# A convolution and mixture-of-experts kernel: the third sort's scatters leave one by one instead of six in a row

## The chip, the cores and the metric

The kernel runs on one core of one Trainium2 chip. The metric is device time in microseconds (us) of one execution; lower is better. The core has TensorE (PE, matrix products and transposes), VectorE (DVE), ScalarE (ACT), GpSimd (POOL) and SyncE (SP, which issues most transfers).

## The reference, cut to what matters

A long convolution over the sequence, by FFT, and then a mixture of experts that sends each token to one expert:

```python
# _attn_ref: x (8, 5696, 128), h (5696, 128)
y = irfft(rfft(x, 2*S) * rfft(h, 2*S))[:, :S, :]
# _moe_ref on the 45568 rows of y: 8 experts, 128 -> 1024 -> 128
logits = x @ w_gate
expert_idx = argmax(logits, axis=1)
gate_w = softmax(logits)[arange(N), expert_idx]
for e in range(8):
    mask = expert_idx == e
    out[mask] = gate_w[mask, None] * (maximum(x[mask] @ w1[e], 0) @ w2[e])
```

## The kernel before, in words

The eight sequences are cut into three groups of 2, 3 and 3. For each group a forward transform (`phase_a`), a product with the filter's spectrum (`phase_b`) and an inverse transform with routing (`phase_c`) follow each other. `phase_c` is the "sort": it makes the convolution's rows, finds each row's expert, and scatters the rows to a table `SR` in HBM in which the rows of an expert lie together. The experts then read tiles of 256 rows from `SR`, and scatter results to `out`.

The third sort has 24 units (`nu`). A unit is six blocks of 120 rows, made in two half units (`nsub` is 2). A half unit is: `synth` on PE (`yp`), `settle` on ACT (copies to `rt`), transposes on PE (`tp`), and `turned`, which splits the transposed rows on ACT (L827) and DVE (L828, then L829) into `y1`, `y2`, `y3`. Per unit `score` makes the logits on PE (`gb`), `route` picks the expert on DVE, and `rank`, a unit later, computes the row numbers `pi` and calls `sort` six times. Each call is one indirect DMA of GpSimd (L687): 120 rows of 130 floats. It waits for the landing of the scatter eight before it (`PIPE_LANES`).

Between two scatters the first and second sorts put a memset on GpSimd (`spent`, of `REST[g]` columns, L920); the third has none, since `QUICK[2]` is 24.

Beside the second and third groups' work runs the stream `experts()`. Its step is a quarter of a tile's hidden layer (256 of 1024 columns): six products `mh` (`layer1`), a relu on ACT (L1200) and a subtraction on DVE (L1202) that make `hs`, and two steps later six products `ma` (`layer2`). Four steps are a tile; its rows are transposed on the way in and out (`mx`). `mh` has two buffers in PSUM, so the products of step k+2 need the relu and the subtraction of step k.

The order of instructions on each engine is fixed when the program is built: `run` takes the next piece of the stream whose running sum of costs is least. After each relu and each subtraction, and after each copy of `phase_b`, `spread` may let one result scatter leave (`place`, L705), with a wait on that instruction; while a sort goes on (`state["space"]`) it does so only with more than `ROOM` results pending.

After the third sort come the fill of `SR`'s free rows, the third part's tables, and the experts alone until the end.

Of the kernel before, what the change touches and what calls it, by code (L numbers as in the profile page):

```python
# [18 lines left out]
ALU = mybir.AluOpType  # L19
# [7 lines left out]
MP = 120  # L27
# [35 lines left out]
ROOM = 28  # L63
REST = (224, 288, 288)
QUICK = (1, 1, 24)
TABLED = 4
RATE = (0.372, 0.55, 0.28, 0.8, 1.05, 0.6)

# [2 lines left out]
def conv_moe(ctx: ExitStack, tc: tile.TileContext, I, out, B, S, D, E, F, split):  # L71
    nc = tc.nc
# [5 lines left out]
    SYNC = mybir.DependencyInfo(mybir.DependencyClass.Sync, mybir.DependencyReason.DATA)  # L78
# [150 lines left out]
    y2 = const.tile([P, max(SLOTS), P], F32, name="y2")  # L229
    y3 = const.tile([P, max(SLOTS), P], BF16, name="y3")  # L230
    for t in (y1, y2, y3):
        nc.vector.memset(t, 0.0)
    y1h, y2h = (t.bitcast(BF16).rearrange("p b (m t) -> p b m t", t=2)[:, :, :, 1] for t in (y1, y2))
# [220 lines left out]
    def phase_b(gr):  # L454
# [154 lines left out]
        def save(n):  # L609
            q, c = items[n]  # L610
            qb, k0 = divmod(q, QB)
            if g == 0:
                nc.scalar.copy(
                    wide[:, q : q + PK], banks.pop(n)[:, : PK * cb * K2].rearrange("p (q b x) -> p q b x", b=cb, x=K2)
                )
                if k0 + PK == QB:
                    tiles.pop(qb), hhs.pop(qb), mats.pop(qb)
                return
            if k0 == 0 and c == 0:
                outs_[qb] = sb.tile([K2, QB, gr.cols], F32, tag="six", name=f"vt{g}_{q}", bufs=SIX)  # L620
            done = nc.scalar.copy(  # L621
                outs_[qb][:, k0 : k0 + PK, c * cw : (c + 1) * cw],
                banks.pop(n)[:K2, :iw].rearrange("p (q x) -> p q x", q=PK),
            )
            spread(done)
            if k0 + PK == QB and c == nch - 1:
                late.append((gr.V[qb * QB : qb * QB + QB].rearrange("q p c -> p q c"), outs_.pop(qb)))
                tiles.pop(qb), hhs.pop(qb), mats.pop(qb)
# [54 lines left out]
    state["w9"] = [const.tile([MP, max(SLOTS), E1], F32, name=f"w9{k}") for k in range(2)]  # L683
    state["base"] = base0

    def sort(pi, rt, b):
        s = nc.gpsimd.indirect_dma_start(  # L687
            out=SR[:, :],
            out_offset=IndirectOffsetOnAxis(ap=pi[:, b : b + 1], axis=0),
            in_=rt[:, b, :],  # L690
            in_offset=None,
            bounds_check=NROWS - 1,
            oob_is_err=False,
        ).ins
        tc.declare_no_dep(s, group="sr", reason="each row of the sorted tokens is written once, before it is read")
        tc.declare_no_dep(s, group="rows", reason="never a row that a tile has read")
        tc.add_to_no_dep_group("sr", s)
        if len(lanes) >= PIPE_LANES:
            tc.add_manual_dep(s, lanes[-PIPE_LANES].name, SYNC, reason="scatter lane")
        lanes.append(s)  # L700

    outs, pending, held = [], [], []

    def place(xr, s, after=None):
        sc = nc.gpsimd.indirect_dma_start(  # L705
            out=out[:, :],
            out_offset=IndirectOffsetOnAxis(ap=xr[:, s, D + 1 : D + 2].bitcast(I32), axis=0),
            in_=xr[:, s, :D],
            in_offset=None,
            bounds_check=B * S - 1,  # L710
            oob_is_err=False,
        ).ins
        tc.declare_no_dep(sc, group="out", reason="each token is written once")
        tc.add_to_no_dep_group("out", sc)
        if len(outs) >= PIPE_LANES:
            tc.add_manual_dep(sc, outs[-PIPE_LANES].name, SYNC, reason="scatter lane")
        if after is not None:
            tc.add_manual_dep(sc, after.name, SYNC, reason="results leave one by one")
        outs.append(sc)

    def spread(done, behind=0):
        gap, now = PACE[0 if state["tail"] else 1], state["pe"] + behind
        if now - state["sent"] < gap:
            return
        if len(pending) > (ROOM if state["space"] else 0):
            place(*pending.pop(0), done.ins)
        elif held and not state["space"]:
            place(*held.pop(0), done.ins)
        else:
            return  # L730
        state["sent"] = now
# [5 lines left out]
    def phase_c(pt, guest=None):  # L737
        gr, g, nb, cb, cw, NI, ns = pt.gr, pt.s, pt.nb, pt.cb, pt.cw, pt.ni, pt.ns
# [5 lines left out]
        nu = NB // NI  # L744
# [76 lines left out]
        def turned(n, k):  # L821
            tv = tbank.pop((n, k))[:, : cb * MP].rearrange("p (b m) -> p b m", m=MP)
            bs = slice(k * cb, (k + 1) * cb)
            if g == 0:
                nc.scalar.copy((y1, y2)[n % 2][:, bs, :MP], tv)
                return
            nc.scalar.copy(y1[:, bs, :MP], tv)  # L827
            nc.vector.tensor_tensor(out=y2[:, bs, :MP], in0=y1[:, bs, :MP], in1=y1h[:, bs, :MP], op=ALU.subtract)  # L828
            nc.vector.tensor_tensor(out=y3[:, bs, :MP], in0=y2[:, bs, :MP], in1=y2h[:, bs, :MP], op=ALU.subtract)  # L829

        lgs, cnts = {}, {}
        wv = w3.rearrange("p t e -> p (t e)")
# [64 lines left out]
        def rank(n):  # L897
            rt, oh = rts.pop(n), gates.pop(n)
            tot, pre = cnts.pop(n)
            cum = sb.tile([P, E1 * ns], F32, tag="cum", name=f"cum{g}_{n}")  # L900
            nc.vector.tensor_tensor_scan(out=cum, data0=going[:, :w], data1=tot, initial=0.0, op0=ALU.mult, op1=ALU.add)
            yield
            base = sb.tile([P, E1, ns], F32, tag="base", name=f"base{g}_{n + 1}")
            prev = state["base"].rearrange("p (e o) -> p e o", o=1).broadcast_to([P, E1, ns])
            nc.vector.tensor_tensor(out=base, in0=cum.rearrange("p (e b) -> p e b", b=ns), in1=prev, op=ALU.add)
            state["base"] = base[:, :, ns - 1]
            yield
            rk = sb.tile([MP, E1 * ns], F32, tag="rk", name=f"rk{g}_{n}")
            nc.vector.tensor_tensor(out=rk, in0=pre, in1=base[:MP].rearrange("p e b -> p (e b)"), op=ALU.add)  # L909
            yield  # L910
            nc.vector.tensor_tensor(out=rk, in0=rk, in1=oh.rearrange("p e b -> p (e b)"), op=ALU.mult)
            yield
            pi = sb.tile([MP, ns], I32, tag="pi", name=f"pi{g}_{n}", bufs=6)
            with nc.allow_low_precision("whole numbers"):
                nc.vector.tensor_reduce(out=pi, in_=rk.rearrange("p (e b) -> p b e", b=ns), axis=AX.X, op=ALU.add)
            yield
            for b in range(ns):
                sort(pi, rt, b)
                if n < nu - QUICK[g]:
                    nc.gpsimd.memset(spent[:, : REST[g]], 0.0)  # L920
# [20 lines left out]
        for n in range(n_end + 1):  # L941
            for k in range(nsub):
# [23 lines left out]
                if 0 <= at - TL < total_sub:  # L966
                    turned(*divmod(at - TL, nsub))
                chains = []
                if g and k == nsub - 1 and 0 <= n - 2 < nu:
                    chains.append(rank(n - 2))  # L970
                if k == nsub - 1 and 0 <= n - 1 < nu:
                    chains.append(route(n - 1))
                if k == 0 and n >= (n_end if g else 2):
                    chains.append(rank(n - 2))
# [139 lines left out]
    def experts():  # L1114
# [82 lines left out]
        def relu(j, k):  # L1197
            hp = hbank.pop((j, k))
            hs = sb.tile([P, 2, 2, T], F32R, tag="hs", name=f"hs{j}_{k}", bufs=4)
            done = nc.scalar.activation(hs[:, 0], hp, AF.Relu)  # L1200
            spread(done)
            done = nc.vector.scalar_tensor_tensor(  # L1202
                out=hs[:, 1], in0=hp, scalar=0.0, in1=hs[:, 0].bitcast(F32), op0=ALU.max, op1=ALU.subtract
            )
            spread(done, 650)
            return hs
# [106 lines left out]
    def gather(pt, guest=None):  # L1313
# [6 lines left out]
        if pt is parts[-1]:  # L1320
            for cost in fill(pt):
                next(pt.pieces, None)
                yield cost
            for _ in range(TABLED):
                next(pt.pieces, None)
# [153 lines left out]
```

## Time and profile before

| | |
|---|---|
| median of 3 runs | 2219.41 us (2211.24 to 2219.84) |
| the profiled execution | 2227.33 us, of which the span is 2225.5 us |
| TensorE busy, mean granted clock | 94% of the span, 0.966 |
| VectorE, ScalarE, GpSimd busy | 70%, 50%, 58% |
| indirect scatters to `SR` / to `out` | 384 / 308 |

The span is the time from the first to the last instruction of the profiled execution. All durations further down come from this execution. An engine that is little busy may still decide when another goes on; so the waits have to be read beside the busy shares.

### The profile page before, as it was taken

To read this page: it belongs to the slowest core of one execution; us is meant where nothing else is said; L and a number is where in the kernel's file an instruction comes from. 1 tells how busy PE (TensorE), PEld (TensorE's weight loads), DVE (VectorE), ACT (ScalarE), POOL (GpSimd) and SP (SyncE) were. 2 spreads that over 40 slices of the span, in tenths; PEclk is the share of its full clock that TensorE was granted. 3 is DMA by queue.
4 is the path that set the end of the run, shared out by engine and by line. 5 is a ranking of instruction groups with operands and counts; after the bars stand their busy time and mean duration, and the time that the engine had idled before them with its cause. 6 is when DMAs were issued, how large, how long until landed. Compare 5 with 4: busy or idle time off the path is not lost.

```text
span 2225.5 us, 47244 instructions
## 1 busy us (share of the span) xinstructions
PE 2093.7 (94%) x14548; PEld 1809.9 (81%) x14548; DVE 1565.7 (70%) x3526; ACT 1118.6 (50%) x2333; POOL 1290.2 (58%) x1431
## 2 busy tenths in 40 slices
PE   9899999799998998989999999888888999999998
PEld 7788777477777776778888888676767999999998
DVE  5588677899995777898887885555655555555554
ACT  5677555255554544436665664333333444444444
POOL 6466478455552588879987771454543444444333
PEclk9999999699999999999999999999989999999999
DMA  8899798988896897777776865455524144333331
GB/s 266 235 286 292 232 304 270 242 236 219 234 255 164 234 272 234 237 201 189 182 216 162 217 191 150 139 143 134 151 73 137 56 129 131 129 129 126 119 119 36
DMA packets 215137, 415.62 MB, mean 187 GB/s; under 512 B 31797, under 2 KB 135531, under 8 KB 214884
## 3 DMA queue, kind: packets, MB, share of 16 engines
q1 hardware_dynamic: 186703, 357.00, 57.0%
q0 software_dynamic: 27072, 55.35, 8.6%
q8 instruction: 118, 1.93, 0.4%
q14 instruction: 135, 1.11, 0.2%
q10 hardware_dynamic: 1109, 0.23, 0.1%
HBM read 571.44 MB, written 154.27 MB: 326 GB/s over the span
## 4 chain that ended last, share of the span: by engine, by line
PE 46%; DVE 3%; issue 1%; another core or an unknown queue 1%; ACT 1%; DMA 1%; POOL 0%; SPq 0%; ACTq 0%; POOLq 0%; DVEq 0%
PE mh L165 18%; PE ma L165 17%; PE mx L190 3%; PE vp L165 3%; PE xp L165 3%; PE yp L165 2%; DMA wb<-WD 1%; ACT hs L1200 1%; DVE hs L1202 0%; PE gb L165 0%; DVE y L829 0%; DVE y L828 0%; PE tp L190 0%; DMA SR<-rt,pi 0%
## 5 line engine op out<-in xcount | busy, mean ns | idle before, releaser
L1202 DVE SCALAR_TENSOR_TENSOR hs<-mh,hs 128x512 fp32r<-128x512 f32 x728 | 500.6, 689 | 425.5 <-ACT hs L1200 352.4
L165 PE MATMUL mh<-xtb,wb 128*128 128x256 f32 x4368 | 710.9, 298 | 35.0 <-DVE hs L1202 17.9
L1200 ACT ACTIVATE hs<-mh 128x512 fp32r<-128x512 f32 x728 | 434.2, 598 | 527.8 <-PE mh L165 403.3
L165 PE MATMUL ma<-hs,wb 128*128 128x256 f32 x4368 | 667.1, 289 | 13.7 <-issue 7.3
L165 PEld LDWEIGHTS mh<-xtb,wb 128*128 128x128 f32 x4368 | 592.9, 191 | 105.5 <-issue 40.3
L165 PEld LDWEIGHTS ma<-hs,wb 128*128 128x128 f32 x4368 | 581.6, 193 | 15.7 <-issue 8.0
L687 POOL DMA_INDIRECT SR<-rt,pi x384 | 395.7, 1031 | 309.1 <-ACT hs L1200 74.5
L705 POOL DMA_INDIRECT out<-xr x308 | 302.7, 983 | 352.1 <-ACT hs L1200 168.5
L584 POOL TENSOR_TENSOR zt<-zt,xs 128x384 f32<-128x384 f32 (+1 forms) x276 | 295.6, 1073 | 159.0 <-DVE xs L574 100.8
L578 DVE TENSOR_TENSOR xs<-xp,hh 64x384 f32<-64x384 f32 (+1 forms) x360 | 214.8, 597 | 7.8
L621 ACT COPY vt<-vp 96x384 f32<-96x384 f32 x240 | 113.9, 475 | 193.2 <-PE vp L165 178.4
L165 PE MATMUL vp<-zt,mi 128*96 128x384 f32 x480 | 200.3, 499 | 0.0
L569 DVE TENSOR_TENSOR zt<-xp,hh 128x384 f32<-128x384 f32 (+1 forms) x300 | 173.6, 579 | 29.6 <-PE xp L165 22.2
L165 PE MATMUL xp<-uq,mt 96*128 96x384 f32 (+1 forms) x496 | 177.9, 463 | 7.4 <-DMA uq<-U 3.5
L165 PE MATMUL pa<-xc,fcr 120*120 120x512 f32 x576 | 159.7, 411 | 4.8 <-DVE ut L330 1.6
L165 PE MATMUL yp<-vq,gcs 120*120 120x384 f32 x384 | 145.8, 502 | 5.5 <-issue 3.0
L574 DVE SCALAR_TENSOR_TENSOR xs<-xp,hh 64x384 f32<-64x384 f32 x240 | 134.3, 559 | 4.2
L165 PEld LDWEIGHTS pa<-xc,fcr 120*120 120x120 f32 x576 | 98.5, 184 | 29.6 <-DVE rk L909 4.8
L165 PEld LDWEIGHTS vp<-zt,mi 128*96 128x96 f32 x480 | 79.7, 167 | 49.6 <-issue 28.3
L330 DVE COPY ut<-pa 120x512 f32<-120x512 f32 x96 | 65.6, 683 | 76.1 <-PE pa L165 48.4
L165 PEld LDWEIGHTS xp<-uq,mt 96*128 96x128 f32 x496 | 88.2, 201 | 32.4 <-issue 14.0
L558 POOL TENSOR_TENSOR us<-uq,us 96x384 fp32r<-96x384 f32 x81 | 83.1, 1026 | 36.7 <-ACT us L556 35.8
(168 smaller groups left out, 2604.8 us busy)
## 6 DMA issues: line engine op xcount, KB each, us to landing
wb<-WD SPq DMA_DIRECT2D x728, 512.0 KB
U<-ut SPq DMA_DIRECT2D x48, 720.0 KB
uq<-U SPq DMA_DIRECT2D x60, 576.0 KB
V<-vt SPq DMA_DIRECT2D x60, 576.0 KB
vq<-V SPq DMA_DIRECT2D x48, 720.0 KB
xt<-x SPq DMA_DIRECT2D x96, 240.0 KB
xr<-SR SPq DMA_DIRECT2D x154, 130.0 KB
WD<-wsp SPq DMA_DIRECT2D x32, 512.0 KB
```

The lines of the kernel that those rows point to most:

```text
L165: nc.tensor.matmul(to, lhs, rhs, **kw)
L190: nc.tensor.transpose(dst, src, ident[:n, :n])
L558: eng.tensor_tensor(out=uv[:, 1], in0=src, in1=uv[:, 0].bitcast(F32), op=ALU.subtract)
L569: nc.vector.tensor_tensor(out=zt, in0=x3, in1=hv[:, 0].broadcast_to([P, PK, cb, D]), op=ALU.mult)
L574: nc.vector.scalar_tensor_tensor(out=xs[to, 0], in0=x3[at, 0], scalar=-1.0, in1=him[:, 0], op0=ALU.mult, op1=ALU.mult)
L578: nc.vector.tensor_tensor(out=xs[to], in0=x3[at], in1=him, op=ALU.mult)
L584: eng.tensor_tensor(out=zt, in0=zt, in1=xs, op=ALU.add)
L621: done = nc.scalar.copy(outs_[qb][:, k0 : k0 + PK, c * cw : (c + 1) * cw], banks.pop(n)[:K2, :iw].rearrange("p (q x) -> p q x", q=PK),)
L687: s = nc.gpsimd.indirect_dma_start(out=SR[:, :], out_offset=IndirectOffsetOnAxis(ap=pi[:, b : b + 1], axis=0), in_=rt[:, b, :], in_offset= ...
L705: sc = nc.gpsimd.indirect_dma_start(out=out[:, :], out_offset=IndirectOffsetOnAxis(ap=xr[:, s, D + 1 : D + 2].bitcast(I32), axis=0), in_=x ...
L1200: done = nc.scalar.activation(hs[:, 0], hp, AF.Relu)
L1202: done = nc.vector.scalar_tensor_tensor(out=hs[:, 1], in0=hp, scalar=0.0, in1=hs[:, 0].bitcast(F32), op0=ALU.max, op1=ALU.subtract)
```

## The change

A list `sorting` is put between `rank` and `sort` for the third sort (`EVEN`). `rank` appends the unit's six scatters to it. While it holds any, each relu of the expert steps takes one from it and issues it with a wait on that relu (the call of `spread` behind the subtraction does nothing then), and so does the last DVE split of each half unit (`turned`, L829 before). What is left of the unit before last is issued by `rank` without a wait, and the last three units' scatters are issued in a row at the end. While the list holds any, `spread` places no results.

```diff
--- before.py
+++ after.py
@@ -63,6 +63,7 @@
 ROOM = 28
 REST = (224, 288, 288)
 QUICK = (1, 1, 24)
+EVEN = (False, False, True)
 TABLED = 4
 RATE = (0.372, 0.55, 0.28, 0.8, 1.05, 0.6)
 
@@ -683,7 +684,9 @@
     state["w9"] = [const.tile([MP, max(SLOTS), E1], F32, name=f"w9{k}") for k in range(2)]
     state["base"] = base0
 
-    def sort(pi, rt, b):
+    sorting = []
+
+    def sort(pi, rt, b, after=None):
         s = nc.gpsimd.indirect_dma_start(
             out=SR[:, :],
             out_offset=IndirectOffsetOnAxis(ap=pi[:, b : b + 1], axis=0),
@@ -697,6 +700,8 @@
         tc.add_to_no_dep_group("sr", s)
         if len(lanes) >= PIPE_LANES:
             tc.add_manual_dep(s, lanes[-PIPE_LANES].name, SYNC, reason="scatter lane")
+        if after is not None:
+            tc.add_manual_dep(s, after.name, SYNC, reason="sorted rows leave one by one")
         lanes.append(s)
 
     outs, pending, held = [], [], []
@@ -720,6 +725,10 @@
 
     def spread(done, behind=0):
         gap, now = PACE[0 if state["tail"] else 1], state["pe"] + behind
+        if sorting:
+            if not behind:
+                sort(*sorting.pop(0), done.ins)
+            return
         if now - state["sent"] < gap:
             return
         if len(pending) > (ROOM if state["space"] else 0):
@@ -826,7 +835,9 @@
                 return
             nc.scalar.copy(y1[:, bs, :MP], tv)
             nc.vector.tensor_tensor(out=y2[:, bs, :MP], in0=y1[:, bs, :MP], in1=y1h[:, bs, :MP], op=ALU.subtract)
-            nc.vector.tensor_tensor(out=y3[:, bs, :MP], in0=y2[:, bs, :MP], in1=y2h[:, bs, :MP], op=ALU.subtract)
+            done = nc.vector.tensor_tensor(out=y3[:, bs, :MP], in0=y2[:, bs, :MP], in1=y2h[:, bs, :MP], op=ALU.subtract)
+            if sorting:
+                sort(*sorting.pop(0), done.ins)
 
         lgs, cnts = {}, {}
         wv = w3.rearrange("p t e -> p (t e)")
@@ -914,6 +925,13 @@
             with nc.allow_low_precision("whole numbers"):
                 nc.vector.tensor_reduce(out=pi, in_=rk.rearrange("p (e b) -> p b e", b=ns), axis=AX.X, op=ALU.add)
             yield
+            if EVEN[g]:
+                while len(sorting) > (ns if n < nu - 2 else 0):
+                    sort(*sorting.pop(0))
+                sorting.extend((pi, rt, b) for b in range(ns))
+                while sorting and n >= nu - 2:
+                    sort(*sorting.pop(0))
+                return
             for b in range(ns):
                 sort(pi, rt, b)
                 if n < nu - QUICK[g]:
```

The order of instructions is the same on all five engines. On GpSimd only the waits of the third sort's scatters differ. The rows below are GpSimd's, in its program order; `DMASW0` to `DMASW7` are the lanes of its own transfers, `DVE` and `Activation` the progress of VectorE and ScalarE, and `rt_5` and `pi_5` belong to unit 5. First unit 5 before:

```order
L687 DMA SR<-rt_5_20704,pi_5_21185 366848x130 [waits DMASW4_49,DVE_49,Activation_49]
L687 DMA SR<-rt_5_20704,pi_5_21185 366848x130 [waits DMASW5_49]
L687 DMA SR<-rt_5_20704,pi_5_21185 366848x130 [waits DMASW6_49]
L687 DMA SR<-rt_5_20704,pi_5_21185 366848x130 [waits DMASW7_49,Activation_49]
L687 DMA SR<-rt_5_20704,pi_5_21185 366848x130 [waits DMASW0_49]
L687 DMA SR<-rt_5_20704,pi_5_21185 366848x130 [waits DMASW1_49]
```

and after the change:

```order
L690 DMA SR<-rt_5_20689,pi_5_21179 366848x130 [waits DMASW4_49,DVE_49]
L690 DMA SR<-rt_5_20689,pi_5_21179 366848x130 [waits DMASW5_49,Activation_49]
L690 DMA SR<-rt_5_20689,pi_5_21179 366848x130 [waits DMASW6_49,Activation_49]
L690 DMA SR<-rt_5_20689,pi_5_21179 366848x130 [waits DMASW7_49,DVE_49]
L690 DMA SR<-rt_5_20689,pi_5_21179 366848x130 [waits DMASW0_49,Activation_49]
L690 DMA SR<-rt_5_20689,pi_5_21179 366848x130 [waits DMASW1_49,Activation_49]
```

The six scatters of before wait once for their unit's data, and after the change each waits for a step of ACT or DVE. Over units 0 to 20, 122 of 126 scatters have such a wait, 79 of them on ACT. On GpSimd again, the last three units; first two whole rows of unit 21 and the start of unit 22 before:

```order
L687 DMA SR<-rt_21_23703,pi_21_24167 366848x130 [waits DMASW4_49,DVE_49,Activation_49]
L687 DMA SR<-rt_21_23703,pi_21_24167 366848x130 [waits DMASW5_49]
L687 DMA SR<-rt_21_23703,pi_21_24167 366848x130 [waits DMASW6_49]
L687 DMA SR<-rt_21_23703,pi_21_24167 366848x130 [waits DMASW7_49,Activation_49]
L687 DMA SR<-rt_21_23703,pi_21_24167 366848x130 [waits DMASW0_49]
L687 DMA SR<-rt_21_23703,pi_21_24167 366848x130 [waits DMASW1_49]
L687 DMA SR<-rt_22_23900,pi_22_24348 366848x130 [waits DMASW2_49,DVE_49,Activation_49]
L687 DMA SR<-rt_22_23900,pi_22_24348 366848x130 [waits DMASW3_49]
```

and after the change, with the end of unit 20 ahead of them:

```order
L690 DMA SR<-rt_20_23490,pi_20_23949 366848x130 [waits DMASW2_49,Activation_49]
L690 DMA SR<-rt_20_23490,pi_20_23949 366848x130 [waits DMASW3_49]
L690 DMA SR<-rt_21_23673,pi_21_24149 366848x130 [waits DMASW4_49]
L690 DMA SR<-rt_21_23673,pi_21_24149 366848x130 [waits DMASW5_49]
L690 DMA SR<-rt_21_23673,pi_21_24149 366848x130 [waits DMASW6_49]
L690 DMA SR<-rt_21_23673,pi_21_24149 366848x130 [waits DMASW7_49]
L690 DMA SR<-rt_21_23673,pi_21_24149 366848x130 [waits DMASW0_49]
L690 DMA SR<-rt_21_23673,pi_21_24149 366848x130 [waits DMASW1_49]
L690 DMA SR<-rt_22_23870,pi_22_24327 366848x130 [waits DMASW2_49,DVE_49]
L690 DMA SR<-rt_22_23870,pi_22_24327 366848x130 [waits DMASW3_49]
```

The scatters of units 21 to 23 have no wait on a step after the change; the first row of units 22 and 23 still waits for their row numbers.

## Rows read from the trace of the kernel before

**Rows 1.** The page: busy us of each engine, share of the span, instructions.

```profile
PE 2093.7 (94%) x14548; PEld 1809.9 (81%) x14548; DVE 1565.7 (70%) x3526; ACT 1118.6 (50%) x2333; POOL 1290.2 (58%) x1431
```

**Rows 2.** Six stretches: us, busy us of each engine, PEclk, DMA share, GB/s.

```profile
640.00:800.00 160.00, 150.96 (x996) 118.22 (x994) 119.75 (x304) 75.10 (x165) 82.06 (x105) 0.98 0.78 216
800.00:976.00 176.00, 152.76 (x1090) 119.47 (x1088) 139.33 (x454) 74.64 (x174) 148.13 (x213) 0.97 0.78 230
1000.00:1330.00 330.00, 326.46 (x2184) 285.79 (x2183) 275.01 (x506) 210.54 (x428) 277.59 (x290) 0.99 0.74 193
1393.15:1667.50 274.35, 229.26 (x1760) 194.38 (x1760) 155.77 (x535) 92.84 (x226) 136.57 (x133) 0.92 0.48 128
1667.50:1690.00 22.50, 12.32 (x80) 11.86 (x80) 9.55 (x37) 4.26 (x9) 11.95 (x12) 0.74 0.23 63
1690.00:2225.50 535.50, 529.16 (x4482) 528.27 (x4480) 299.83 (x531) 260.38 (x516) 219.34 (x226) 1.00 0.35 113
```

**Rows 3.** Waits of 1393.15 to 1667.5: total us, times, longest us.

```profile
DVE hs L1202 <- ACT hs L1200: 80.4, 24, 6.3
...
ACT hs L1200 <- PE mh L165: 60.9, 28, 5.8
```

**Rows 4.** Timeline of one unit's six scatters: start us, us, what, idle before.

```profile
1505.50 1.00 POOL L687 DMA_INDIRECT SR<-rt,pi  x1 [3.15 <-ACT xtb L1184]
...
1510.10 0.96 PE L165 MATMUL mh<-xtb,wb 128*128 128x256 f32 x6
...
1512.31 1.00 POOL L687 DMA_INDIRECT SR<-rt,pi  x1 [0.30 <-issue]
...
1514.12 0.77 SPq L1163 DMA_DIRECT2D wb<-WD  x2
...
1514.19 0.60 ACT L1200 ACTIVATE hs<-mh 128x512 fp32r<-128x512 f32 x1 [6.14 <-remote]
```

**Rows 5.** Timeline of the last scatters of the third sort.

```profile
1681.81 1.00 POOL L687 DMA_INDIRECT SR<-rt,pi  x1 [0.30 <-issue]
...
1683.81 0.60 ACT L1200 ACTIVATE hs<-mh 128x512 fp32r<-128x512 f32 x1 [7.90 <-remote]
```

**Rows 6.** Rows of L687 and L705 on POOL, third sort: times ns, first and last start.

```profile
L687 POOL DMA_INDIRECT SR<-rt,pi x144: 992/1000/1370, 1393.1 to 1681.8; - x144
...
L705 POOL DMA_INDIRECT out<-xr x6: 967/992/993, 1333.1 to 1354.4; - x6
```

**Rows 7.** Groups of ACT in 1720 to 1900; of ACT, then PE, in 1393.15 to 1667.5.

```profile
L1200 ACT ACTIVATE hs<-mh 128x512 fp32r<-128x512 f32 x118 | 70.5, 598 | 88.9 <-PE mh L165 70.3 <-issue 18.2 <-DVE hs L1202 0.3
...
L1200 ACT ACTIVATE hs<-mh 128x512 fp32r<-128x512 f32 x80 | 46.7, 594 | 117.5 <-PE mh L165 60.9 <-remote 25.8 <-PE ma L165 11.8
...
L165 PE MATMUL yp<-vq,gcs 120*120 120x384 f32 x164 | 63.5, 510 | 0.1
...
L190 PE MATMUL tp<-ident,rt 120*128 120x120 f32 x126 | 20.2, 270 | 3.4 <-ACT rt L810 1.8 <-issue 1.5
...
L165 PE MATMUL gb<-w,y 128*128 128x24 bf16 x396 | 13.8, 173 | 2.1 <-issue 2.0
```

**Rows 8.** Line L705 in 1000 to 1330: scatters of results beside the second transform.

```profile
L705 POOL DMA_INDIRECT out<-xr x84: 966/992/1027, 1000.3 to 1327.2; - x84
```

**Rows 9.** POOL in the second sort: two scatters with a memset between them.

```profile
842.05 0.99 POOL L687 DMA_INDIRECT SR<-rt,pi  x1 [0.18 <-issue]
843.05 0.35 POOL L920 MEMSET spent<- 120x288 f32 x1
843.58 1.00 POOL L687 DMA_INDIRECT SR<-rt,pi  x1 [0.18 <-issue]
```

**Rows 10.** POOL in the expert tail: first and last of ten scatters in a row.

```profile
1740.36 0.97 POOL L705 DMA_INDIRECT out<-xr  x1 [1.62 <-DVE hs L1202]
...
1758.72 0.97 POOL L705 DMA_INDIRECT out<-xr  x1 [1.61 <-DVE hs L1202]
```

**Rows 11.** First transposes of the third part's rows, on PE.

```profile
1724.65 0.38 PE L190 MATMUL mx<-ident,xr 128*128 128x128 f32 x2
```

## The prediction

> **What bounds the kernel now.** First the page's busy shares: TensorE (PE) is busy 94% of the span, its weight loads, which overlap, 81%, the next engine 70% [rows 1]. Time is won only where PE stands still or runs at the lower of its two clocks. Then the table by stretches [rows 2]. Beside the second transform PE is busy 326.5 of 330 us at a granted clock of 0.99, and in the experts' tail 529 of 535.5 us at 1.00. The third sort, from its first scatter to that of unit 22, is worse: 229.3 of 274.35 us at a clock of 0.92. So 45 us stand idle there, and part of the rest runs at half clock after the idle stretches. DMA is at 0.48 and VectorE (DVE) at 57%, so neither is full.
>
> Third, who waits for whom in that stretch [rows 3]: DVE's `hs` for the relu 80 us, the relu for PE's `mh` 61 us. PE waits for nobody that is slow; the chain ends at a product of PE that is said to be late. Fourth, one unit in order of time [rows 4]. GpSimd (POOL) issues its six scatters from 1505.50 to 1513.31, one after another. PE starts the six products `mh` at 1510.10 and they end, as modelled, at 1511.06; the relu that needs them starts at 1514.19 after 6.14 us of idling. At 1514.12 SP's weight load, which waits for PE's products too, goes on as well. Two engines that wait for PE are let go together, 0.8 us after the last scatter has ended. The last run of scatters says the same: it ends at 1682.81, and a relu that idled for 7.90 us starts 1.0 us later [rows 5]. I read this so: while scatters follow each other closely, PE's report that products are done comes late, until about 1 us after the last one.
>
> **What a better order can give.** PE's own work in the stretch, at full clock: from the busy time, 229.3 x 0.92 = 211 us. From the pieces: the tail makes a step in 180 / 118 = 1.525 us, so 80 steps are 122 us, and the sort's products `yp`, `tp` and `gb` were busy 63.5 + 20.2 + 13.8 = 97.5 us (not corrected for the clock); 219.5 together [rows 7]. I take 215. The stretch lost 274 - 215 = 59 us, over 22 units 2.7 us each.
>
> **The change, part by part.**
> Instructions: none is added or removed on any engine; the order is the same. 144 scatters of 1.000 us remain [rows 6]; what the `sort` calls cost is unchanged.
> The waits: 122 scatters now wait for a step of ScalarE (ACT) or DVE. Behind a waiting scatter stand only further scatters: no result leaves between 1354.4 us and the end of the sort [rows 6]. So a held POOL delays nobody but the sort's own table. No result loses its place in `spread` either, since none had one there.
> Spacing: six scatters took 7.8 us of a unit of 12.5 us. If a unit shrinks to 215 / 22 = 9.8 us plus what remains lost, say 10.4 us, a scatter leaves every 1.74 us, on the mean, in place of 1.36 us. Two will still come close together where a split follows a relu. But a third cannot pile up while PE's report is held, because the next relu needs that report: the holding ends itself.
> What the new spacing costs PE, from two sides. The best case is the stretch beside the second transform: 84 result scatters [rows 8], and a useful share (busy share times clock) of 0.989 x 0.99 = 0.979. The tail's ten scatters in 18.36 us, 2.04 us apart, leave PE as full [rows 2, 10]. At 0.979 the stretch takes 215 / 0.979 = 220 us: 55 us won. The bad case is the second sort, where a memset holds scatters 1.53 us apart [rows 9]: useful 0.868 x 0.97 = 0.842, against 0.944 x 0.98 = 0.925 in the stretch ahead of it, which has the same forward transform and experts but no sort. So scatters at that distance cost 0.083 [rows 2]. With 0.979 - 0.083 = 0.896 the stretch takes 240 us: 34 us won. By distance, 1.74 us lies nearer to 1.53 than to 2.04; by mechanism the holding that ends itself speaks for the better end. I take the middle, **45 us**.
> The end: units 21 to 23 leave 18 scatters in a row, where before there were 6 and then 12. I take this at nothing: 18 in a row at 1.3 us are 23.5 us of POOL either way, and the 22.5 us after 1667.5 lose about as much as now [rows 2]. If the longer run holds PE once more, it costs some 6 us, as in [rows 5]. The sort may end up to one unit's scatters (8 us) later relative to the steps; the third part's rows are first needed on PE at 1724.65, 42 us after the last scatter's end [rows 5, 11], which covers that.
> Buffers: `rt` and `pi` have six buffers and are held for up to one unit longer, three or four units instead of two or three. If that cover were gone, `settle` would wait for a landing, and with it PE's transposes.
>
> The sum, for the profiled execution: 2227.3 - 45 = 2182 us. That execution is 7.9 us above the median of the runs shown, 2219.4; so for the median 2219.4 - 45 = **2174 us**.
>
> **A rule that speaks against it.** The rows show PE's dependents released only after the scatters [rows 4, 5]. The Trainium skill ("SBUF — State Buffer", Who interferes with whom) says that only the port pair shared by VectorE and GpSimd causes contention, that DMA never contends with a compute engine, and that PE and ACT never wait on anyone. By that, scatters in flight would not hold PE, and the coincidence in the rows would need another cause. The trace speaks against a literal reading, with 3.1 us from the products' end to the relu; it does not name the mechanism. What the rule would make of the time is the second rival.
>
> **The rivals.**
> 1. *The scatters stay too close* (chance 0.17). Pairs and triples behind neighbouring steps hold PE as in the second sort, with that stretch's whole useful share: 215 / 0.842 = 255 us, 19 us won, 2200 us. For it: the distance is only 1.74 against 1.53 us, and four scatters in the middle and 18 at the end have no new wait. Against it: part of that share is lost without a sort as well (0.925).
> 2. *Scatters are not what holds PE* (0.12): the late report comes from something that goes with a unit of the sort, such as its chains between PE, ACT and DVE, and the distance of scatters changes nothing. Time 2219 us, within 11 us. For it: no row shows what holds the report. Against it: the release comes 0.8 and 1.0 us after a run's last scatter both times [rows 4, 5].
> 3. *Slower* (0.07): the scatter now starts just as a relu ends, that is, when PE works on the products the next relu needs, and every scatter holds that report for its own 1.0 us and 0.8 us more. A step behind a relu of 0.6 us would take at least 0.05 + 0.6 + 1.0 + 0.8 = 2.45 us against 1.525; 79 such steps cost 73 us, and 215 + 73 = 288 us is 14 us more than now: 2233 us. It decides from (274 - 215) / 79 = 0.75 us per relu with a scatter. Against it: the stretch beside the second transform loses 3.5 us of PE with 84 single scatters [rows 2, 8], 0.04 us each; and PE has the products of an earlier step and of the sort to do meanwhile.
>
> **How the numbers follow.** The forecast's own case, 30 to 63 us won (2156 to 2189), has 0.64: its lower bound lies a little under the 34 us of the bad case, the upper is all that was lost by the smaller count of PE's work. With the first rival's 0.17 the range 2154 to 2204 us holds 0.81. About 0.5%, 11 us, is what a measurement of this kernel tells from no change. Faster by more: 0.64 + 0.17 = 0.81; within it 0.12; slower 0.07.
>
> **What the profile after would show.** Right: in the third sort PE's useful share near 0.94 or above with a clock near 1.00; the stretch from first scatter to that of unit 22 near 229 us; POOL's `SR` scatters with idle time ahead of most, ended by ACT's `hs` or DVE's `y`; no relu that idles over 4 us except at the end, behind the row of 18; the tail and everything ahead of 1393 us unchanged. Wrong: relus that idle 5 to 7 us though scatters stand apart (rival 2); POOL rows still in threes and fours with 0.30 us between (rival 1); a wait of one to two us at nearly each step, starting where a scatter starts (rival 3); or PE waiting in the tail for rows of `SR`, which would mean that the end of the sort has become late.

## The result and the profile after

The change takes 2184.47 us (median of 6 runs, 2177.47 to 2191.45), the kernel before 2219.62 us beside it (6 runs, 2207.99 to 2224.89). The ratio is 0.9845, 95% interval 0.9821 to 0.9869: 35 us faster. The profiled execution took 2177.47 us, its span is 2175.6 us.

The page after, same line as [rows 1] (busy us, share of the span, instructions):

```profile
PE 2067.3 (95%) x14548; PEld 1787.0 (82%) x14548; DVE 1566.0 (72%) x3526; ACT 1119.1 (51%) x2333; POOL 1286.9 (59%) x1431
```

To see where the time came from, I cut both profiles at the same steps of ACT (its 2333 instructions have the same order in both). The first cut is a step beside the first scatter of the sort, the last is the step at which the third part's rows are first needed [rows 11]. In the kernel before the three pieces hold the scatters of units 0 to 6, 7 to 16, and 17 to 23; in the change up to five scatters fewer have left by the same step. The table by stretches (us; busy us of PE, PEld, DVE, ACT, POOL; PEclk; DMA share; GB/s), before:

```profile
1393.80:1481.00 87.20, 73.19 (x568) 61.69 (x566) 49.88 (x172) 30.23 (x74) 43.04 (x43) 0.94 0.47 124
1481.00:1604.20 123.20, 103.95 (x808) 88.31 (x808) 70.67 (x243) 42.17 (x105) 61.96 (x60) 0.93 0.54 142
1604.20:1724.60 120.40, 98.19 (x746) 89.62 (x747) 67.47 (x201) 41.40 (x91) 52.17 (x52) 0.89 0.39 118
```

and after:

```profile
1374.00:1447.20 73.20, 67.74 (x568) 57.34 (x566) 49.88 (x172) 30.21 (x74) 39.18 (x40) 1.00 0.57 148
1447.20:1553.20 106.00, 98.82 (x808) 82.86 (x808) 70.86 (x243) 42.71 (x105) 57.09 (x58) 0.98 0.61 161
1553.20:1674.60 121.40, 94.01 (x748) 85.71 (x748) 67.15 (x201) 41.34 (x92) 57.55 (x58) 0.92 0.39 121
```

The pieces do not agree. The first wins 14.0 us and the second 17.2 us: PE's busy share rises from 0.84 to 0.93 in both, and the granted clock from 0.94 and 0.93 to 1.00 and 0.98. The last piece wins nothing, 121.4 against 120.4 us. Of the 49.9 us between the two profiled executions, 19.8 us already lay ahead of 1393.8 us, in parts of the program that are the same; so this pair shows 30.2 us from the sort, where the medians differ by 35.

The waits after, in the whole sort (total us, times, longest us), against [rows 3]:

```profile
DVE hs L1220 <- ACT hs L1218: 62.5, 22, 8.4
ACT hs L1218 <- PE mh L166: 55.3, 28, 4.6
...
POOL SR L690 <- issue: 23.5, 73, 0.7
...
ACT hs L1218 <- remote: 19.9, 3, 14.5
```

The chain of waits has kept its form and lost part of its length. Of 144 scatters 73 still start with no wait of their own (119 before), 53 of them ahead of a row at the end; where relus come late, several scatters find theirs already done and leave together. One relu idled for 14.5 us. That is at the end, on the timeline (start us, us, what, idle before):

```profile
1600.67 1.00 POOL L690 DMA_INDIRECT SR<-rt,pi  x1 [0.30 <-issue]
...
1602.88 27.73 SPq L1181 DMA_DIRECT2D wb<-WD  x4
...
1609.80 1.00 POOL L690 DMA_INDIRECT SR<-rt,pi  x1 [0.30 <-issue]
...
1626.36 0.60 ACT L1218 ACTIVATE hs<-mh 128x512 fp32r<-128x512 f32 x1 [14.48 <-remote]
1626.76 1.00 POOL L690 DMA_INDIRECT SR<-rt,pi  x1 [0.30 <-issue]
1627.73 1.36 PEld L166 LDWEIGHTS mh<-xtb,wb 128*128 128x128 f32 x6 [13.97 <-issue]
1627.74 1.65 PE L166 MATMUL mh<-xtb,wb 128*128 128x256 f32 x6 [13.77 <-issue]
```

Here 22 scatters, four left over from unit 20 and the 18 of the end, follow each other at 1.3 us, and none behind the first waits for a step. Some relus still go on inside the row, at 1602.95 and 1609.45 us; then PE stands still for 13.8 us, and SP's group of four weight loads stretches over 27.73 us. The relu that idled for 14.48 us goes on 1.4 us ahead of the row's end at 1627.76. Some 20 us later the DMA queues are nearly full, PE falls below its share of 9.80 in the 10 us before 1650, and the idle time ahead of its products ends with a weight load's landing:

```profile
1650.00:1660.00 10.00, 8.86 (x75) 8.68 (x75) 4.52 (x8) 4.57 (x10) 3.92 (x4) 1.00 0.25 74
1660.00:1670.00 10.00, 8.59 (x69) 8.00 (x67) 4.79 (x10) 3.91 (x9) 3.88 (x4) 1.00 0.92 302
```

```profile
1655.58 0.95 PE L166 MATMUL mh<-xtb,wb 128*128 128x256 f32 x6 [1.14 <-DMA wb<-WD]
...
1663.23 0.94 PE L166 MATMUL mh<-xtb,wb 128*128 128x256 f32 x6 [1.26 <-DMA wb<-WD]
```

These waits are for the most part not the row's doing. The same sixteen steps of ACT in the kernel before, in the change, and in the change on a second chip, where no scatter holds anything (f0 below):

```profile
1708.32:1724.63 16.31, 16.31 (x139) 16.15 (x138) 8.93 (x15) 8.22 (x17) 7.35 (x8) 1.00 0.92 312
1653.76:1674.57 20.81, 17.85 (x142) 16.88 (x141) 9.06 (x16) 8.22 (x17) 7.35 (x8) 1.00 0.73 252
1606.88:1626.41 19.53, 17.44 (x142) 16.78 (x141) 9.05 (x16) 8.22 (x16) 7.34 (x8) 1.00 0.75 263
```

In the twelve profiles of the experiments these steps take 19.0 to 20.9 us, with rows and without. Only the kernel before takes 16.3; no run tells why.

### The profile page after: what moved, and what is told of

The parts are those of the page before. It is cut to its first block, busy times and chain, and to the rows that moved or that the text cites. A ratio compares the mean times of both kernels' runs of the same rounds, so it can differ in the third digit from the quotient of the medians.

```text
span 2175.6 us, 47320 instructions
## 1 busy us (share of the span) xinstructions
PE 2067.3 (95%) x14548; PEld 1787.0 (82%) x14548; DVE 1566.0 (72%) x3526; ACT 1119.1 (51%) x2333; POOL 1286.9 (59%) x1431
## 4 chain that ended last, share of the span: by engine, by line
PE 78%; DVE 7%; DMA 5%; issue 4%; ACT 3%; SPq 2%; POOL 1%; another core or an unknown queue 0%; DVEq 0%; ACTq 0%; POOLq 0%
PE mh L166 21%; PE ma L166 20%; PE vp L166 8%; PE xp L166 8%; PE yp L166 5%; PE pa L166 5%; PE mx L191 3%; DMA wb<-WD 2%; PE lb L191 1%; DMA mt<-mq 1%; PE tp L191 1%; PE hp L166 1%; PE gb L166 1%; PE gb_None L166 1%; DVE y L838 1%
## 5 line engine op out<-in xcount | busy, mean ns | idle before, releaser
L166 PE MATMUL ma<-hs,wb 128*128 128x256 f32 x4368 | 656.5, 286 | 5.1 <-DMA wb<-WD 4.2
L166 PEld LDWEIGHTS ma<-hs,wb 128*128 128x128 f32 x4368 | 572.4, 190 | 6.7 <-DMA wb<-WD 5.6
```

Source lines behind the costliest of these rows:

```text
L166: nc.tensor.matmul(to, lhs, rhs, **kw)
```

## The experiments

**Theory:** scatters in a close row hold the reports of PE and ACT until about 1 us after the row; the change wins what its spacing avoids, and its own row of 18 gives some back. **Rivals:** something else that goes with a unit is late, whatever the scatters do; or the place behind a relu counts, not the distance.

**End spread (e1).** Against the change, the last three units' scatters leave one by one as well, and what is left is issued behind the sort:

```diff
-                while len(sorting) > (ns if n < nu - 2 else 0):
+                while len(sorting) > (ns if n < nu - 2 else 2 * ns):
                     sort(*sorting.pop(0))
                 sorting.extend((pi, rt, b) for b in range(ns))
-                while sorting and n >= nu - 2:
-                    sort(*sorting.pop(0))
                 return
...
+        while sorting:
+            sort(*sorting.pop(0))
```

> The change, but the last three units' scatters too leave behind relus; at most the three that are left when the third part begins go out in a row. Theory A (scatters in a close row hold PE's report that products are done): the row of 18 cost about 9 us in the changed kernel (between the same two relus the lead over the kernel before falls by 5 us beside the row and by 4 us in the weight loads behind it), so this one is 7 to 11 us faster than the change: 2174 to 2178 where the change has 2184, and no relu idles over 4 us near the end. Theory B (something that goes with a unit of the sort holds PE, not the scatters' distance): the same time as the change, 2184 within 4, and the long idling of a relu stays at the end.

**Six behind a relu (e2).** The first relu takes all that the list holds, so that there are rows of six again, placed as the change places its first:

```diff
         if sorting:
             if not behind:
                 sort(*sorting.pop(0), done.ins)
+                while sorting:
+                    sort(*sorting.pop(0))
             return
...
-            if sorting:
-                sort(*sorting.pop(0), done.ins)
```

> Each unit's six scatters leave in a row again, but all six behind the first relu after their row numbers, so the wait on a relu is kept and the spacing is undone. Theory A: the row holds PE as before, 2210 to 2225, with a relu that idles 4 to 7 us in most units. Theory B (the wait on a relu and the later start are what helps): 2180 to 2190.

**Memset (e3).** The kernel before, with the memset of the other sorts between the third sort's scatters:

```diff
-QUICK = (1, 1, 24)
+QUICK = (1, 1, 1)
```

> The kernel before with the second sort's memset between the third sort's scatters: 1.53 us from start to start, GpSimd never idle, no wait on a relu. Theory A with distance alone as the measure: most of the gain at 1.53 us, 2188 to 2200 (the prediction's bad case was 34 us won). Theory A with the self-ending wait as the measure (the next scatter has to wait for PE's report): little gain, 2205 to 2220. Theory B: 2215 to 2225.

**Pairs (e4).** The change, but each second event (a relu or a split) releases two scatters:

```diff
-                sort(*sorting.pop(0), done.ins)
+                release(done)
...
+    def release(done):
+        turns_taken[0] += 1
+        if turns_taken[0] % 2 == 0:
+            sort(*sorting.pop(0), done.ins)
+            if sorting:
+                sort(*sorting.pop(0))
```

> The change, but every second relu or split lets two scatters go in a row, with none at those between; the end is that of the change. Theory A: rows of two hold PE for little more than singles, since the first 2 us of a row of six were seen to pass; between the change and the kernel before but near the change, 2184 to 2198. Theory B: 2180 to 2190.

These four ran on one chip, and there the kernel before took 2138.44 us (31 runs), 81 us less than in the first measurement. e1 took 2136.13 us (ratio 0.9988, 0.9969 to 1.0006), e2 2136.84 (0.9995, 0.9978 to 1.0013), e3 2137.54 (1.0000, 0.9984 to 1.0016), e4 2138.13 (1.0004, 0.9987 to 1.0020). None is to be told from before. Every expectation that gave the placements different times missed; what the runs told was that the loss itself was not there.

**The change once more, and three of these, on a second chip.** Is it the chip, or are these kernels all alike for another reason? The change itself takes the place of the pairs.

> The changed kernel itself, as the base for the other three of this chip. On the chip of the first four runs the kernel before took 2138 us instead of 2219 and no row of scatters held PE's report, so there nothing could be won. Theory A': rows of scatters hold PE's report on some chips and not on others. If the kernel before takes about 2138 here, the change gains nothing (ratio within 0.5% of 1); if it takes 2210 to 2225, the change gives 0.980 to 0.988. Theory B' (the gain measured first was something else than the spacing, such as a chance of that session): ratio within 0.5% of 1 even where the kernel before takes 2210 to 2225.

> The change with the last three units' scatters behind relus too. Theory A' on a chip that holds: 7 to 11 us faster than the change on the same chip, no relu idling over 4 us near the end. On a chip that does not hold: the same as the kernel before within 0.5%, as in the first run of it.

> Six scatters in a row behind one relu. Theory A' on a chip that holds: the gain is undone, 0.995 to 1.003 of the kernel before, with a relu that idles 4 to 7 us in most units. Theory B (the wait on a relu and the later start help, whatever the spacing): 0.980 to 0.988. On a chip that does not hold: 1.000 within 0.5%.

> The kernel before with a memset between the third sort's scatters, 1.53 us from start to start. On a chip that holds: if distance is the measure, 0.986 to 0.991; if it is the wait that ends the holding by itself, 0.993 to 1.002. On a chip that does not hold: 1.000 within 0.5%.

Before took 2135.59 us (31 runs), the change 2135.79 (1.0009, 0.9994 to 1.0025), the end spread 2136.41 (1.0004, 0.9988 to 1.0021), six behind a relu 2133.27 (0.9992, 0.9975 to 1.0010), the memset 2137.58 (1.0016, 1.0002 to 1.0030). So the change gains nothing here, which is what was expected of a chip that holds nothing. Its profile from this chip is of the same program as the profile after. The same three pieces:

```profile
1368.60:1437.10 68.50, 67.25 (x570) 57.53 (x570) 50.24 (x173) 30.72 (x74) 39.45 (x40) 1.00 0.60 157
1437.10:1534.10 97.00, 95.22 (x808) 81.34 (x806) 70.55 (x244) 43.15 (x105) 56.86 (x57) 1.00 0.66 179
1534.10:1626.40 92.30, 87.16 (x747) 80.88 (x747) 66.25 (x199) 41.35 (x91) 57.02 (x58) 1.00 0.49 155
```

PE is busy 0.98 of the first two pieces at a granted clock of 1.00. And the row of scatters at the end, with the steps beside it:

```profile
1576.20 1.00 POOL L690 DMA_INDIRECT SR<-rt,pi  x1 [0.30 <-issue]
...
1577.51 1.00 POOL L690 DMA_INDIRECT SR<-rt,pi  x1 [0.31 <-issue]
...
1581.55 0.60 ACT L1218 ACTIVATE hs<-mh 128x512 fp32r<-128x512 f32 x1 [1.29 <-PE mh L166]
...
1582.71 1.00 POOL L690 DMA_INDIRECT SR<-rt,pi  x1 [0.30 <-issue]
1582.99 0.60 ACT L1218 ACTIVATE hs<-mh 128x512 fp32r<-128x512 f32 x1 [0.84 <-PE mh L166]
...
1584.02 1.00 POOL L690 DMA_INDIRECT SR<-rt,pi  x1 [0.30 <-issue]
1584.77 0.60 ACT L1218 ACTIVATE hs<-mh 128x512 fp32r<-128x512 f32 x1 [1.18 <-PE mh L166]
```

The scatters are as close as in the first profile, 1.3 us apart, yet a relu starts every 1.4 to 1.8 us between them. Nothing is held. So the pieces of this profile are a measure of what holding costs: before lost 18.7, 26.2 and 28.1 us of its three pieces, 73.0 us in all, and the change loses 4.7, 9.0 and 29.1 us. The records of the semaphores differ too. If each instruction is given the next recorded update of its semaphore, 95 of 100 reports of PE in the third sort came within some 3.3 us of the modelled end of the instruction in the kernel before, within 2.1 us in the profile after, and within 0.02 us here; for ACT it is 5.3, 3.7 and 0.01 us.

These times are upper bounds, though, as a report whose record is missing counts as late. Of PE's 2431 reports the traces of the kernel before, of the change and of h1 below have 2133, 2127 and 2135, those of the eleven other runs 2418 or more. In the tail, where no time is lost, 95 of 100 of before's reports come within 1.2 us by the same count. The lost time is told by the idling of relus and PE; that just the profiles which lose it also lack an eighth of PE's records is a second difference between the chips.

**Three ways in one program (g1).** As chips differ, the ways to place scatters were put in one program, so that one profile would compare them: units 0 to 7 in rows of six behind a relu, 8 to 15 with a memset behind each, 16 to 23 one by one with the end spread.

```diff
                 sort(*sorting.pop(0), done.ins)
+                while sorting and state["row"]:
+                    sort(*sorting.pop(0))
...
-            if sorting:
+            if sorting and not state["row"]:
                 sort(*sorting.pop(0), done.ins)
...
+                state["row"] = n < 8
+                if 8 <= n < 16:
+                    for b in range(ns):
+                        sort(pi, rt, b)
+                        nc.gpsimd.memset(spent[:, : REST[g]], 0.0)
+                    return
...
```

> All three ways in one third sort, so that one chip shows them side by side: units 0 to 7 six in a row behind one relu, units 8 to 15 with a memset between the scatters and no wait on a relu, units 16 to 23 one behind each relu or split, the end included. Two chips so far let every row pass (before 2138 and 2136 us), the one of the first measurement did not (before 2219 us). Theory A' (rows hold PE's report on some chips): if the kernel before takes 2210 to 2225 here, units 0 to 7 take about as long as before (12.5 us each), units 8 to 15 10.5 to 12, units 16 to 23 10 to 11 and no relu idles over 4 us at the end, and the whole gains 20 to 30 us. If it takes about 2137 here, each unit takes 9.2 to 9.9 us whichever way, and the ratio is 1.000 within 0.5%. Theory C (the holding was of the session of the first measurement, not of a chip) gives the second answer on every chip from now on.

On a third chip it took 2136.49 us against 2134.79 (1.0008, 0.9984 to 1.0031): again a chip that holds nothing, and no answer.

**Double rows (h1).** One program with more of the cause at one place and less at another. Units 0 to 7 write each of their rows a second time, to a table that nobody reads (added work: 48 scatters); units 8 to 15 are placed as before the change; units 16 to 23 leave one by one, the end as in e1.

```diff
+                if n < 16:
+                    for b in range(ns):
+                        sort(pi, rt, b)
+                        if n < 8:
+                            sort(pi, rt, b, to=SR2)
+                    return
...
```

> Adds work: in units 0 to 7 each scatter is followed by a copy of it into a second table that nobody reads, so 12 leave in a row; units 8 to 15 leave six in a row as in the kernel before, units 16 to 23 one behind each relu or split, the end too. Three chips let rows of six pass without a late report. Theory A'' (enough scatters in a row hold the engines' reports on any chip, the first measurement's chip was only nearer to that): in units 0 to 7 reports of PE come 1 us late or more and relus idle 4 to 8 us, in units 8 to 15 not. Theory A' (some chips hold, others never): on a chip with the kernel before at 2137 no report is late by over 0.1 us anywhere, and units 0 to 7 are bound by GpSimd at 12 x 1.3 = 15.6 us each only as far as the six buffers of rt run out, some 10 to 40 us in all; on a chip with the kernel before at 2215 or more, units 0 to 7 are the slowest at over 15 us, units 8 to 15 take 12.5 us, and units 16 to 23 10 to 11 us.

This chip took 2217.91 us for the kernel before (3 runs, 2216.32 to 2222.39), and 2271.47 us for h1 (2 runs): ratio 1.0237, 1.0197 to 1.0277. The three pieces of its profile, cut at the same steps of ACT; the first holds the 96 scatters of units 0 to 7:

```profile
1380.00:1549.20 169.20, 86.48 (x583) 69.28 (x582) 51.13 (x173) 31.21 (x75) 96.12 (x96) 0.72 0.33 84
1549.20:1672.20 123.00, 105.84 (x792) 88.92 (x792) 70.88 (x244) 42.02 (x104) 55.95 (x55) 0.89 0.54 140
1672.20:1770.30 98.10, 89.69 (x748) 82.33 (x747) 66.46 (x199) 41.28 (x91) 51.45 (x52) 0.98 0.46 142
```

The first piece takes 169.2 us where before took 87.2 for the same steps. GpSimd's own work does not explain all of that: twelve scatters at 1.3 us are 15.6 us a unit, 125 us for eight, which leaves 44 us, and it is busy 96 of the 169 us. What the added scatters alone cost was not measured, since no chip that holds nothing ran this program. The relu's group in that piece and its longest kind of wait (idle us ahead of the group, by what ended it):

```profile
L1225 ACT ACTIVATE hs<-mh 128x512 fp32r<-128x512 f32 x26 | 15.5, 597 | 107.0 <-remote 84.9 <-PE mh L167 14.8 <-PE ma L167 5.2
```

and one row of twelve with the relus on both sides of it:

```profile
1405.01 0.60 ACT L1225 ACTIVATE hs<-mh 128x512 fp32r<-128x512 f32 x1 [0.50 <-PE mh L167]
1406.24 1.00 POOL L691 DMA_INDIRECT SR<-rt,pi  x1 [0.30 <-issue]
...
1407.19 0.95 PE L167 MATMUL mh<-xtb,wb 128*128 128x256 f32 x6
...
1415.38 1.00 POOL L691 DMA_INDIRECT SR<-rt,pi  x1 [0.30 <-issue]
1417.88 1.09 SPq L1188 DMA_DIRECT2D wb<-WD  x3
1417.95 0.60 ACT L1225 ACTIVATE hs<-mh 128x512 fp32r<-128x512 f32 x1 [12.35 <-remote]
```

The products end at 1408.14, the row at 1416.38, and relu and weight load go on 1.5 us after that: twice the row, twice the wait of [rows 4], and released after the row's end again. Not every release waits for that: of 20 places in the third sort of the kernel before where ACT idles over 3.5 us, 14 go on 0.4 to 1.4 us after a row has ended, and 6 go on 0.6 to 7.5 us ahead of its end.

From first scatter to first scatter, units 0 to 7 take 22.3 us each, where before took 12.7. Units 8 to 15, placed as before, take 12.7 us where the profile of before has 12.3 and the change on the second chip 10.4: the loss of the first measurement is back. (That the second piece takes 123.0 us, as against 123.2, is in part chance: it holds 55 scatters here and 59 there.) Units 16 to 22, one by one, take 10.9 us. All three are what was expected of a chip that holds. And the last piece, with the scatters of units 17 to 23, takes 98.1 us, where before took 120.4 and the change 121.4. Within one program, on one chip, the loss follows the length of the rows. Whether rows of twelve would hold reports on a chip that lets rows of six pass was not tried.

**Two more attempts at a direct time of the end spread and of the three ways (i1, j1),** the kernels of e1 and g1 on two further chips.

> Only the end differs from the change: the last three units' scatters leave one by one too. If the kernel before takes about 2218 us on this chip (rows hold reports here): by my theory the change's gain of 35 us and some 15 to 20 us more, 2163 to 2170 us, with no ACT idle over 5 us in the third sort and none of 14 us behind its end. By the rival that the end was bound by its weight loads, 2180 to 2186 us. If the kernel before takes about 2136 us here, nothing holds a report and both theories expect no difference: within 0.3%.

> One program, three ways of spacing: units 0 to 7 of the third sort send their six scatters in a row, but as soon as behind a relu; units 8 to 15 put a memset behind each; units 16 to 23 leave one by one, the last three too. If the kernel before takes about 2218 us on this chip, then by my theory the first part takes what the kernel before takes there (some 12.4 us a unit), the second about 11.4 and the third about 10.5 us a unit, and the whole 2180 to 2200 us; by the rival that only the distance between scatters of a row of many counts, all three take the same. If the kernel before takes about 2136 us here, all three take some 9.5 to 10 us a unit and the whole is within 0.3%.

Both chips hold nothing: i1 2134.70 us against 2135.68 (0.9995, 0.9976 to 1.0015), j1 2135.23 against 2135.30 (1.0003, 0.9986 to 1.0021). The pieces of j1, in the main with six behind a relu, memsets, and singles:

```profile
1373.70:1442.20 68.50, 67.45 (x572) 57.75 (x571) 50.19 (x173) 30.83 (x75) 43.62 (x43) 1.00 0.63 160
1442.20:1539.20 97.00, 95.17 (x807) 81.28 (x805) 70.64 (x244) 43.06 (x105) 77.58 (x108) 1.00 0.66 181
1539.20:1631.90 92.70, 87.19 (x747) 80.87 (x747) 66.31 (x199) 41.42 (x91) 51.56 (x52) 1.00 0.47 149
```

To 0.4 us they are those of the change on the second chip, whatever the placement. Where nothing is held, PE is busy 0.98 of the first two pieces, and the distance of scatters is worth nothing.

## Why the prediction was right, point by point

- **What bounds the kernel:** right on the chip of the first measurement. The step "PE's report that products are done comes late, until about 1 us after the last" scatter is borne out by h1: rows twice as long, waits of 12.35 us in place of 6.14, released 1.5 us after the row. It is wider than I put it, since reports of ACT come late as well, and less strict, since 6 of 20 releases come ahead of a row's end. That the loss belongs to some chips alone was not foreseen: on the second chip the same forecast would have been wrong, with 2135.79 us for the change and 2135.59 for the kernel before.
- **What was lost:** 59 us to unit 22's scatter. The same stretch of the change on the second chip took 210.4 us against before's 273.4, so it was 63; PE's work was put a little too high at 215 us.
- **The spacing, 45 us:** mis-sized by 5. Until the end row of scatters begins, the lead over before grows from 19.8 to 59.3 us, 39.5 us won. By the scatters themselves, from the first to that of unit 22, the stretch takes 239.1 us where I had 229; there unit 22's scatter already stands in the end row. The step that was too hopeful is "the holding ends itself": ahead of the end row 53 of 122 scatters still start without a wait, and the first two pieces still lose 13.7 of 44.9 us. PE's useful share there, busy share times clock, is 0.925 and 0.91, where I wrote 0.94 or above and where the second chip has 0.98. This is nearer to the bad case of 0.896 than to the best, but that is luck, for the 0.083 of the bad case is not the price of scatters 1.53 us apart. The second sort and the stretch ahead of it, at the same steps of ACT in the change on the second chip, where nothing is held:

```profile
629.40:783.70 154.30, 148.32 (x990) 116.72 (x988) 118.91 (x303) 74.56 (x165) 80.49 (x104) 0.99 0.79 223
783.70:952.40 168.70, 151.52 (x1095) 119.97 (x1096) 142.04 (x460) 74.70 (x174) 147.76 (x212) 0.97 0.79 236
```

The useful share falls from 0.95 to 0.87 there, by 0.08 as well, so most of what I laid to the scatters belongs to something else in the second sort.
- **The end, at nothing:** the term that failed. It "loses about as much as now" was wrong by 5 us; the lead falls from 59.3 us to 54.1 across the row. From the last relu ahead of the end to one well behind it (1595.8 to 1637.8 us in the change), the same steps take 36.9 us in the kernel before, 42.0 in the change, 21.4 in h1, whose end is spread, and 19.6 on the second chip. I had allowed the 6 us of one more hold and then put the term at nothing. Another 4 us of the lead, to 50.1, go between 1653.8 and 1674.6 us, where PE waits for weight loads; I had not named them, and at most 1 of them can be the row's, as the second chip pays 3 without any holding. By 42.0 against 21.4 us, leaving the end in a row costs the change some 20 us.
- **The sum:** 45 for 30 us in this pair of profiles, which is 39.5 less 5.2 for the end and 4.1 for the weight loads; 35 by the medians, so 2184 us in place of 2174, inside the range. Why the medians differ by 5 us more than the sort in this pair is not shown. Ahead of the sort, where I expected no change, the pair differs by 19.8 us; that is no effect of the change, since the programs are the same there.
- **Covers:** right. From the first step of the tail that needs the third part's rows on, the lead stays at 50.1 to 49.9 us; no row of `SR` was late, and no buffer.
- **"Every relu's idle under 4 us but at the end":** nearly, the longest on `mh` is 4.6 us.
- **Rival 1, too close:** part of it is true, since scatters still come in short rows, nine of them of three to six ahead of the end, but 35 us were won instead of 19. **Rival 2, not the scatters:** falls by h1. **Rival 3, a wait at each step:** does not show; in h1 scatters follow relus one by one and the piece takes 98.1 us against 92.3 without any holding, 6 us in all.
- **The rule of the Trainium skill** ("SBUF — State Buffer", Who interferes with whom), that PE and ACT never wait on anyone and DMA never contends with a compute engine, speaks of the ports of SBUF: five of seven measurements agree with it, in that nothing is lost beside rows of scatters, and on the second chip 95 of 100 reports came within 0.02 us. Two do not, with relus that idle up to 14.5 and 22.2 us beside rows of scatters. The measurement decides for those; it does not say that a port is what is held. The Trainium skill ("Perfetto Trace Analysis", Tensor Engine Instruction) says too that a matmul's end is an estimate and that its semaphore update comes after it. The trace agrees: the update can follow the modelled end within 0.02 us, as on the second chip, and in [rows 4] relu and weight load go on 3.1 us after it.

**What stays open.** What it is in a chip or a session that makes rows of scatters hold reports, and which part of it is held, no run here tells. All timed runs here carry a span and a clock from the profiler, and the profiles that lose time are those that lack records; whether the recording is itself what is held up, and whether an execution without it loses the time as well, was not tried. Whether the wait on a relu does more than distance alone would (the rival of the memset) met only chips without holding. And the end spread was never timed by itself where it should gain: 2184 - 20 = 2164 us is an estimate from the end of h1's sort.

## What to carry to other kernels

Where an engine waits for a product that ended long ago, look at what the other queues do until it goes on: here a row of GpSimd scatters had ended some 1 us before at 14 of 20 such places, and was still going on at the others. Space such scatters among the steps, and do it for the last ones too, since one long row cost some 20 us, about half of what the twenty units ahead of it won. And measure on more than one chip before a gain of this kind is called one: here it is 1.5% on one chip and nothing on the other one that ran it, so the change is a guard, not a gain everywhere.

## What was not expected of the hardware

The kernel before takes 2135 to 2138 us on five chips and 2218 to 2220 us in two measurements, each within 0.6% of its median. Of the 98.1 us between its profile and that of the change on the second chip, 73.0 lie in the third sort, 25.3 ahead of it and none in the tail behind. The 25.3 us cannot be put to holding: on chips that hold nothing the third sort begins at 1368.6 to 1383.1 us, and the change and h1, on chips that hold, begin it at 1374.0 and 1380.0. PE's granted clock falls with the idling, to 0.72 on the mean in h1's first piece, where PE is busy 86 of 169 us; so a held report costs twice, as idle time and as work at the lower of its two levels (the six products `mh` took 1.65 us after the standstill of 13.8 us, and 0.95 us at 1655.58).
